# Scores in groups of eight and values in groups of eight once the maxima are through, in a gated mix of linear and softmax attention

## The chip, the cores and the metric

The kernel runs on one core of a Trainium2 chip. The metric is the device time of one execution, in microseconds (us). The kernel before takes 1025.13 us, the median of 3 runs (1024.96 to 1025.58). The engines are named as the profile names them: PE is TensorE (matmuls; PEld are its weight loads), DVE is VectorE, ACT is ScalarE, POOL is GpSimd, and SP is SyncE, whose queue issues the DMA transfers (SPq).

## The reference, cut to what matters

```python
B, S, D, H = 1, 2048, 448, 16          # Dh = 28

def _A_ref(x, wqkv, w_phi, wo):        # linear attention with learned features
    q, k, v = split(x @ wqkv)
    pq, pk = q @ w_phi, k @ w_phi      # per head
    phi_q = concat([softmax(pq), softmax(-pq)])
    phi_k = concat([softmax(pk), softmax(-pk)])
    kv, z = phi_k.T @ v, phi_k.sum(over s)
    return heads_joined((phi_q @ kv) / (phi_q @ z + 1e-6)) @ wo

def _B_ref(x, wqkv, wo):               # full softmax attention
    q, k, v = split(x @ wqkv)
    p = softmax(q @ k.T * Dh ** -0.5)
    return heads_joined(p @ v) @ wo

g = sigmoid((x * gate_w).sum(-1, keepdims=True))
out = g * _A_ref(x, A_wqkv, A_w_phi, A_wo) + (1 - g) * _B_ref(x, B_wqkv, B_wo)
```

All inputs and the output are 32-bit floats. The change touches only the second half of the softmax attention (B) and its output projection.

## The kernel before, in words

The first 440 us or so compute the projections of x, the linear attention A with its output (kept in DRAM as `gad`, one block of 512 tokens each), the values of B (`vb`), and the queries and keys of B, which are stored in DRAM (`qkd`).

Then comes the long loop at the end of the function, over steps `s`. A step is one tile of 128 keys (`kt`, 16 of them) for one block `gq` of four heads and 512 queries: `g` counts four groups of four heads, `qb` four blocks of queries, `gq = 4 g + qb`. There are 256 steps (`NS`). A step has these parts, in this order on TensorE:

- Scores (`scores`, L865): four matmuls of 128x128 against 128x512, one per head (L871). Each writes a PSUM bank of its own, taken from the list `free`; when a step's four are issued, its banks go back to the list's end. ScalarE then takes the exponential of each bank (L889) into a tile `p`; `p` has eight buffers, two steps' worth.
- Values (`values`, L991) of the step before: per head a 32-column matmul on the exponentials (L998). A 32-bit product takes two passes, so these are eight matmuls of 128x32 against 128x512, in two groups of four that run side by side on the four column quarters of the array. They add into one bank, `pv`, over the block's 16 steps. A column of ones among the values gives the sum of the exponentials.
- Maxima (`mx_visit`, L304): a step's share of the row maxima of later blocks (L321, four matmuls), read by ScalarE (L325) and VectorE (L329, L332). They are through at step 212. Until then their query and key tiles (`qc`, `kc`, from `mx_tile`, L178) are in use; after that they are idle. `spare_open` (L942) then returns their banks and keeps one, the spare, for projections, so that scores cycle through six.

A finished block goes through `finish` (L1035), called with the number `s` of the step at which the block's last values are issued. `f1` at once: VectorE copies `pv` (L398), SP sends the sums' rows to a small tile (L401). `f2` at `s + 3`: VectorE takes the reciprocals (L408), SP writes them to DRAM (L412) and reads them back spread over the partitions (L413). `f3` at `s + 8`: GpSimd multiplies (L419). `f4` at `s + 9`, issued at the next step's start: GpSimd splits the result into a high and a low part (L427, L428); for the first three groups of heads SP stores them (L1055, `od`).

When the last group of heads of a query block is through (blocks 12, 13, 14), its 512 tokens are projected in four pieces (`project`, L1003): eight passes on the stored heads of the other groups (`first_passes`, L1013), then three on the fresh ones (`out_passes`), eleven matmuls of 128x128 against 128x448 (L108) into the spare bank; VectorE adds the gated result (L1009) and SP sends it (L1011). The pieces are issued at steps `s + 10` to `s + 13`, that is 218 to 221, 234 to 237 and 250 to 253, behind the step's values. The stored heads are loaded by `load_out` (L951), seven DMA issues at the steps in `OUTS`: blocks 0, 1 and 2 share one buffer (`oL`), block 3 has the idle buffer `kst[1]` and a tile `oLl`. Block 15, the last, is finished in the tail (`tail_open`, `tail_fill`, `finish_last`, from L1019 on).

The order of the work on TensorE, VectorE, ScalarE and GpSimd is the order in which the code is written. SP's queue is ordered by a planner at build time: it places a DMA issue as soon as, by its reckoning, what the issue needs is ready, and among several that are ready it takes the one that stands first in the code. A transfer can thus be issued many steps ahead of its place. At run time SP works through its queue in order.

The loop's lines that the change rewrites:

```python
            if s:
                scores(s, 0)
                scores(s, 1)
        ...
        if 0 < s <= NS:
            values(s - 1)
```

Of the kernel before, what the change touches and what calls it, by code (L numbers as in the profile page):

```python
# [8 lines left out]
F32 = mybir.dt.float32  # L9
# [8 lines left out]
P = 128  # L18
# [5 lines left out]
NG = 4  # L24
NT = S // P
NQ = S // 512
# [2 lines left out]
NU = NG * NQ * 16  # L29
NF = 44  # L30
LOWEST = -3.0e38
OUTS = (200, 222, 242, 206)


def f32(ap):
    return ap.bitcast(F32)
# [3 lines left out]
def gated_mix_kernel(ctx, tc, xT, wqkB, wvB, wvA, wkAT, wqAT, phi, woA, woB,  # L40
# [26 lines left out]
    def ps_mx(nm, d):  # L67
        return ps.tile([P, 2, 512], F32, tag="md" if d and psn[1] == 3 else "mx", name=nm,
                       bufs=1 if d and psn[1] == 3 else 2)
# [36 lines left out]
    def run(dst, todo):  # L106
        for i, (l, r) in enumerate(todo):
            nc.tensor.matmul(dst, l, r, start=i == 0, stop=i == len(todo) - 1)  # L108
# [48 lines left out]
    acts = []  # L157
# [6 lines left out]
    def take_acts():  # L164
        while acts:
            acts.pop(0)()
# [11 lines left out]
    def mx_tile(tag, nm, bufs):  # L178
        return mxp.tile([P, 512], F32R, tag=tag, name=nm, bufs=bufs)
# [214 lines left out]
    def normalize1(pool, pn, nm, n):  # L394

        oU = pool.tile([P, n, 512], F32, tag="oU", name=f"oU{nm}", bufs=1 + n)
        for i in range(n):
            (nc.scalar.copy if n == 2 else nc.vector.tensor_copy)(oU[:, i, :], pn[i])  # L398
        den = pool.tile([P, n, 16], F32, tag="den", name=f"den{nm}", bufs=2)
        for i in range(n):  # L400
            nc.sync.dma_start(den[:, i, :], oU[DH:P:32, i, :])  # L401
        return oU, den
# [29 lines left out]
    def out_passes(oT, c, w, g):  # L432
        tt = slice(c, c + P)
        return [(oT[:, 0, tt], w[:, 0, g, :]), (oT[:, 0, tt], w[:, 1, g, :]),
                (oT[:, 1, tt], w[:, 0, g, :])]
# [290 lines left out]
    for i in range(2 * NT + 11):  # L726
        t, q = i, i - NT
# [132 lines left out]
        kst_of[(g, kb)] = load_stack(kst[(4 * g + kb) % 5], k_d[g], kb * 512, (0, 1, 0, 1))  # L860

    NS = NG * NQ * NT
    pv_of, pts, late, mids = {}, {}, {}, {}

    def scores(s, i):  # L865

        gq, kt = divmod(s, NT)
        g, qb = divmod(gq, NQ)

        def score(j, st):  # L870
            nc.tensor.matmul(st, kst_of[(g, kt // 4)][:, j, (kt % 4) * P:(kt % 4 + 1) * P],  # L871
                             qst_of[gq][:, j, :], start=True, stop=True)

        if s == 0:
            p = at.tile([P, 2, 512], F32, name=f"p{s}_{i}")
            st = ps_mx(f"st{s}_{i}", i)
            for jl in range(2):
                score(2 * i + jl, st[:, jl, :])
            nc.scalar.activation(p, st, AF.Exp, scale=SCALE)
            pts.setdefault(s, []).extend([p[:, 0, :], p[:, 1, :]])  # L880
            return
        sts = []
        for j in (2 * i, 2 * i + 1):
            used.append(free.pop(0))
            sts.append(bank(used[-1], f"st{s}_{j}"))
            score(j, sts[-1])
        for st in sts:
            p = late_p.tile([P, 512], F32, tag="p", name=f"p{s}_{len(pts.get(s, []))}", bufs=8)
            nc.scalar.activation(p, st, AF.Exp, scale=SCALE)  # L889
            pts.setdefault(s, []).append(p)  # L890
        if i == 1:
            a, m = used[:], held[:]
            free.extend([a[0], m[0], a[1], m[1], a[2], a[3], m[2]] if m else a)
            used.clear()
            held.clear()
# [33 lines left out]
    free, used, held = list(range(7)), [], []  # L929
    spare = []  # L930

    def bank(i, nm):
        return ps2.tile([P, 512], F32, tag=f"g{i}", name=nm, bufs=1)
# [8 lines left out]
    def spare_open():  # L942
        free.extend(held)
        held.clear()
        spare.append(free.pop())

    late_p = ctx.enter_context(tc.tile_pool(name="late", bufs=1, reuse_waits="tile"))
    woB_s = late_p.tile([P, 2, 4, D], F32R, name="woB_s")
# [2 lines left out]
    def load_out(qb):  # L951


        if qb < NQ - 1:
            o = late_p.tile([P, NG - 1, 2, 512], F32R, tag="oL", name=f"oL{qb}", bufs=1)
            oL_of[qb] = [o[:, b] for b in range(NG - 1)]
        else:
            o = kst[(4 * NG) % 5]
            oL_of[qb] = [o[:, 0:2], o[:, 2:4],
                         late_p.tile([P, 2, 512], F32R, tag="oLl", name="oLl", bufs=1)]  # L960
        tt = slice(qb * 512, (qb + 1) * 512)
        for b in range(2):
            nc.sync.dma_start(f32(oL_of[qb][b]), o_d[b * P:(b + 1) * P, :, tt])
        r = oL_of[qb][2]
        for i in range(2):
            nc.sync.dma_start(f32(r[:80, i, :]), o_d[256:336, 0, tt])
        nc.sync.dma_start(f32(r[80:, 0, :]), o_d[288:336, 1, tt])
        nc.sync.dma_start(f32(r[80:96, 1, :]), o_d[288:304, 1, tt])
        nc.sync.dma_start(f32(r[96:, 1, :]), o_d[256:288, 1, tt])
# [33 lines left out]
    def project(qb, oT, tl):  # L1003

        t = qb * 4 + tl
        acc = acc_of[qb][:, tl, :]
        po = bank(spare[0], f"pob{t}")
        run(po[:, :D], first_passes(qb, tl) + out_passes(oT, tl * P, woB_s, NG - 1))
        nc.vector.scalar_tensor_tensor(acc, po[:, :D], gate1[:, t:t + 1], acc,  # L1009
                                       op0=ALU.mult, op1=ALU.add)  # L1010
        nc.sync.dma_start(out[0, t * P:(t + 1) * P, :], acc)  # L1011

    def first_passes(qb, tl):  # L1013
        o, tt = oL_of[qb], slice(tl * P, (tl + 1) * P)
        return [x for b in range(2) for x in out_passes(o[b], tl * P, woB_s, b)] + [
            (o[2][:, i, tt], woB_s[:, i, 2, :]) for i in range(2)]
# [3 lines left out]

    def tail_open():
        tail["po"] = [bank(i, f"poL{n}")[:, :D]
                      for n, i in enumerate([spare[0], free.pop(0), free.pop(0)])]
        for tl in range(4):
            tail["todo"] += [(tl, i == 0, x) for i, x in enumerate(first_passes(NQ - 1, tl))]

# [8 lines left out]
    def finish(gq, s):  # L1035

        st = {}
        g, qb = divmod(gq, NQ)
        last = gq == NG * NQ - 1

        def f1():
            st["n"] = normalize1(late_p, [pv_of[gq]], f"b{gq}", 1)

        def f2():
            st["n"] = normalize2(late_p, *st["n"], f"b{gq}", 1, False)

        def f3():
            st["n"] = normalize3(*st["n"], 1)

        def f4():  # L1050
            st["o"], = normalize4(late_p, st["n"], f"b{gq}", 1)
            if g < NG - 1:
                for j in range(4):
                    r = (4 * g + j) * DH
                    nc.sync.dma_start(o_d[r:r + DH, :, qb * 512:(qb + 1) * 512],  # L1055
                                      f32(st["o"][32 * j:32 * j + DH]))

        if last:
            finish_last(gq)
            return  # L1060
        f1()
        late.setdefault(s + 3, []).append(f2)
        late.setdefault(s + 8, []).append(f3)
        late.setdefault(s + 9, []).append(lambda: acts.append(f4))
        if g == NG - 1:
            for tl in range(4):
                mids[s + 10 + tl] = lambda tl=tl: project(qb, st["o"], tl)

    def finish_last(gq):

# [43 lines left out]

    for s in range(NS + 16):
        take_acts()
        if s < NS:
            gq, kt = divmod(s, NT)
            g, qb = divmod(gq, NQ)
            if s in (0, 3):  # L1120
                load_k(0, 2 + s // 3)
            if g + 1 < NG and qb == NQ - 1 and kt % 4 == 2:
                load_k(g + 1, kt // 4)
            if kt == 12 and gq + 1 < NG * NQ:
                load_q(gq + 1)
            if kt == (12 if gq + 1 < 14 else 14) and gq + 1 < NG * NQ - 1:
                load_nm(gq + 1)
            if s in OUTS:
                load_out(OUTS.index(s))
            if g == NG - 1 and kt == 8:  # L1130
                load_acc(qb)
            if s:
                scores(s, 0)
                scores(s, 1)
        if s == NS:
            tail_open()
            tail_fill(3)
        if 0 < s <= NS:
            values(s - 1)
            if s % NT == 0:  # L1140
                finish(s // NT - 1, s)
        if s:
            mx_visit()
        if mxs["f"] == len(flats):
            mx_fin()
        if s in mids:
            mids.pop(s)()
        if mxs["f"] == len(flats) and not spare:
            spare_open()
        if NG * NQ - 1 in nm_of and NG * NQ - 1 in qst_of:  # L1150
            load_nm(NG * NQ - 1)
        for fn in late.pop(s, []):
            fn()
# [68 lines left out]
```

## Time and profile before

| what | us |
|---|---|
| median of 3 runs | 1025.13 |
| the profiled execution | 1025.96 |
| its span | 1024.2 |
| step 213's scores begin | 889.80 |
| step 214's scores begin | 891.97 |
| first projection's matmuls begin | 902.57 |
| tail begins (first matmul of L1032) | 1007.91 |
| last matmuls of scores before the tail begin | 1005.79 |

The span is the time from the first to the last instruction of the profiled execution. Busy time of PE is modelled: matmuls are pipelined, and a row's length includes its way through the array, so the distance between the starts of two rows says more than their lengths. A row of the timeline is start, length, engine, line, operation, output and inputs, shapes, count, and in brackets the idle time before it on that engine with what ended it.

### The profile page before, as it was taken

The numbers are of one execution on the slowest core, as the hardware profiler recorded it, in microseconds if no ns is written. First come the engines' busy times: TensorE is split into PE (matmuls) and PEld (weight loads), VectorE is DVE, ScalarE is ACT, GpSimd is POOL, SyncE is SP. The second block draws the span as 40 slices with busy tenths as digits, with TensorE's granted clock in tenths as the row PEclk, the third lists the DMA queues.
The fourth block names the chain that finished last, engine by engine and source line by source line (L and its number), as shares of the span: only waits on it lengthen the run. The fifth ranks groups of instructions, "written<-read, shape, count | busy, mean of one in ns | idle before, by whom it ended". The sixth has DMA issues, their size and how long they took to land.

```text
span 1024.2 us, 18042 instructions
## 1 busy us (share of the span) xinstructions
PE 1013.9 (99%) x6472; PEld 557.3 (54%) x6472; DVE 680.7 (66%) x1340; ACT 820.0 (80%) x1534; POOL 236.2 (23%) x213
## 2 busy tenths in 40 slices
PE   9999999999999999999999999999999999999998
PEld 8878888868779433333333333333333333354555
DVE  6566567987753588788888787887878887710102
ACT  5445445677752999999999999999999999969672
POOL 1245546678435003111011110101201101011010
PEclk9999999989999999999999999999999999999999
DMA  8973110132345713233532133522313355414401
GB/s 297 310 238 93 52 52 1 61 73 81 94 129 132 146 26 77 69 68 72 123 79 72 42 74 74 128 58 55 89 42 77 87 129 140 121 58 125 132 32 54
DMA packets 64250, 98.89 MB, mean 97 GB/s; under 512 B 18176, under 2 KB 24944, under 8 KB 64160
## 3 DMA queue, kind: packets, MB, share of 16 engines
q1 hardware_dynamic: 64160, 97.74, 35.4%
q8 instruction: 51, 0.84, 0.4%
q14 instruction: 39, 0.32, 0.1%
HBM read 69.54 MB, written 27.78 MB: 95 GB/s over the span
## 4 chain that ended last, share of the span: by engine, by line
PE 89%; DVE 4%; DMA 4%; ACT 1%; SPq 1%; issue 1%; POOL 0%; DVEq 0%; ACTq 0%; POOLq 0%
PE st L871 29%; PE pv L998 25%; PE pm L321 9%; PE pk L126 4%; PE pva L126 4%; PE poa L108 4%; PE pob L108 3%; PE pq L108 2%; PE pqk L108 2%; DMA qkd<-ev 2%; PE pvb L126 2%; PE pvb L108 2%; PE pmb L284 1%; PE pft L524 1%; DVE rl L289 1%; DMA wvA_raw<-in_wvA_dram 1%
## 5 line engine op out<-in xcount | busy, mean ns | idle before, releaser
L889 ACT ACTIVATE p<-st 128x512 f32<-128x512 f32 x1020 | 525.7, 609 | 29.5 <-PE st L871 27.9
L332 DVE TENSOR_REDUCE part<-pm 128x1 f32<-128x512 f32 x477 | 304.8, 686 | 111.1 <-PE pm L321 104.7
L871 PE MATMUL st<-qst,kst 128*128 128x512 f32 x1024 | 315.5, 430 | 0.5 <-ACT vb L714 0.5
L998 PE MATMUL pv<-p,vb 128*32 128x512 f32 x2048 | 272.7, 605 | 0.0
L871 PEld LDWEIGHTS st<-qst,kst 128*128 128x128 f32 x1024 | 173.0, 187 | 137.5 <-issue 75.8
L321 PEld LDWEIGHTS pm<-kc,qc 28*128 28x128 f32 x848 | 40.5, 181 | 177.8 <-ACT p L889 169.4
L325 ACT ACTIVATE rl<-pm 128x512 f32<-128x512 f32 x212 | 126.9, 599 | 11.0 <-PE pm L321 0.3
L419 POOL TENSOR_TENSOR oUb<-oUb,rsb 128x512 f32<-128x512 f32 x15 | 19.3, 1289 | 467.4 <-DMA rsb<-rdb 229.9
L329 DVE CUSTOM_DVE_ANT_0 rl<-pm,rl 128x512 f32<-128x512 f32 x159 | 108.3, 681 | 0.0
L321 PE MATMUL pm<-kc,qc 28*128 28x512 f32 x848 | 107.1, 495 | 0.0
L998 PEld LDWEIGHTS pv<-p,vb 128*32 128x32 f32 x2048 | 40.3, 108 | 67.3 <-issue 63.1
L289 DVE CUSTOM_DVE_ANT_0 rl<-pmb,rl 128x512 f32<-128x512 f32 x88 | 57.1, 686 | 29.4 <-ACT rl L287 29.4
L1009 DVE SCALAR_TENSOR_TENSOR acc<-pob,gate,acc 128x448 f32<-128x448 f32 x12 | 8.2, 684 | 86.2 <-PE pob L108 86.2
L108 PE MATMUL pqk<-XH,wB 128*128 128x512 f32 x192 | 59.3, 397 | 0.0
L287 ACT ACTIVATE rl<-pmd 128x1024 f32<-128x1024 f32 x44 | 45.2, 1028 | 12.2 <-PE pmd L284 5.6
L588 ACT CAST ev<-pqk 128x512 fp32r<-128x512 f32 x28 | 16.1, 588 | 36.1 <-PE pqk L108 30.2
L108 PE MATMUL poa<-woA_s,oTa 128*128 128x448 f32 x192 | 43.2, 374 | 0.0
L108 PEld LDWEIGHTS pqk<-XH,wB 128*128 128x128 f32 x192 | 35.4, 188 | 8.5 <-issue 1.5
L108 PE MATMUL pq<-wqA_s,XH 128*128 128x448 f32 x128 | 38.1, 381 | 0.8 <-DVE ev L589 0.8
L195 POOL TENSOR_TENSOR kc<-kc,kd 28x512 fp32r<-28x512 f32 x12 | 15.4, 1281 | 101.9 <-PE pm L321 50.7
L108 PEld LDWEIGHTS poa<-woA_s,oTa 128*128 128x128 f32 x192 | 35.1, 188 | 6.0 <-issue 3.3
L589 DVE TENSOR_TENSOR ev<-pqk,ev 128x512 fp32r<-128x512 f32 x28 | 19.0, 690 | 28.4 <-ACT ev L588 28.3
(159 smaller groups left out, 1176.8 us busy)
## 6 DMA issues: line engine op xcount, KB each, us to landing
qkd<-ev SPq DMA_DIRECT2D x28, 512.0 KB
qst<-qkd SPq DMA_DIRECT2D x64, 224.0 KB
kst<-qkd SPq DMA_DIRECT2D x64, 224.0 KB
od<-oTb SPq DMA_DIRECT2D x48, 112.0 KB
rsa<-rda SPq DMA_DIRECT2D x8, 512.0 KB
rsb<-rdb SPq DMA_DIRECT2D x15, 256.0 KB
kc<-qkd SPq DMA_DIRECT2D x64, 56.0 KB
gad<-ga SPq DMA_DIRECT2D x16, 224.0 KB
```

The lines of the kernel that those rows point to most:

```text
L108: nc.tensor.matmul(dst, l, r, start=i == 0, stop=i == len(todo) - 1)
L126: nc.tensor.matmul(dst[:, :n], l, r, start=i == 0, stop=i == len(todo) - 1, skip_group_check=True)
L287: nc.scalar.activation(rl, pd, AF.Relu)
L289: nc.vector.tensor_tensor_reduce(rl[:, i, :], pb[:, i, :], rl[:, i, :], 1.0, LOWEST, ALU.add, ALU.max, part[:, col + i:col + i + 1])
L321: nc.tensor.matmul(pm[j], mxs[("qc", gq)][js, qt * P:(qt + 1) * P], mxs[("kc", g, kb)][js, :], start=True, stop=True, tile_position=(32 * ...
L325: nc.scalar.activation(rl, pm[kb], AF.Relu if kb < 3 else AF.Copy)
L329: nc.vector.tensor_tensor_reduce(r, pm[j], r, 1.0, LOWEST, ALU.add, ALU.max, part[:, col + j:col + j + 1])
L332: nc.vector.tensor_reduce(part[:, col + j:col + j + 1], pm[j], AX.X, ALU.max)
L419: (nc.gpsimd if n == 1 else nc.vector).tensor_mul(oU, oU, rs)
L871: nc.tensor.matmul(st, kst_of[(g, kt // 4)][:, j, (kt % 4) * P:(kt % 4 + 1) * P], qst_of[gq][:, j, :], start=True, stop=True)
L889: nc.scalar.activation(p, st, AF.Exp, scale=SCALE)
L998: nc.tensor.matmul(pv[32 * j:32 * j + 32, :], vb[kt // 8][:, kt % 8, 4 * g + j, :], pt[j], start=kt == 0, stop=kt == NT - 1, tile_position ...
```

## The change

`TWO` is 213, the first step after the last maxima. Up to step 212 nothing is different in the order of scores and values. From step 213 on:

- An odd step issues its own scores and those of the next step, eight matmuls in a row; an even step issues none. Values stay as they were, one step's at each step, so that on TensorE eight scores are followed by two steps' values. The last step, 255, has only its own four.
- The exponentials of odd steps use the tiles `p` as before. Those of even steps use the maxima's idle tiles: `kc` (five buffers) for steps divisible by four, and three of `qc` (three buffers) with one of `kc` for the other even steps.
- No bank is kept as a spare: scores cycle through seven banks. A projection takes the next bank of the same list and puts it at the list's end; the tail takes its banks from the list too.
- The projections are issued at every second step: 218, 220, 222, 224 for block 0, 234 to 240 for block 1, 248 to 254 for block 2, each behind the second of two steps' values.
- For blocks that finish from step 213 on, `f2` is issued at `s + 2` in place of `s + 3`, `f3` and `f4` at `s + 5` in place of `s + 8` and `s + 9`.
- `load_out`: block 1 at step 227 in place of 222, block 2 at 206 in place of 242, block 3 at 243 in place of 206. Block 2 now has the buffers that block 3 had (`kst[1]` and `oLl`), and blocks 0, 1 and 3 share `oL`.

```diff
-OUTS = (200, 222, 242, 206)
+OUTS = (200, 227, 206, 243)
+PROJ = (218, 234, 248)
...
+    TWO = NG * NQ * 16 - NF + 1
...
-        for st in sts:
-            p = late_p.tile([P, 512], F32, tag="p", name=f"p{s}_{len(pts.get(s, []))}", bufs=8)
+        for j, st in enumerate(sts, 2 * i):
+            if s < TWO or s % 2:
+                p = late_p.tile([P, 512], F32, tag="p", name=f"p{s}_{j}", bufs=8)
+            else:
+                tag = "qc" if s % 4 and j < 3 else "kc"
+                p = f32(mx_tile(tag, f"p{s}_{j}", 3 if tag == "qc" else 5))
             nc.scalar.activation(p, st, AF.Exp, scale=SCALE)
...
     def spare_open():
         free.extend(held)
         held.clear()
-        spare.append(free.pop())
+        spare.append(1)
...
-        if qb < NQ - 1:
+        if qb != 2:
             o = late_p.tile([P, NG - 1, 2, 512], F32R, tag="oL", name=f"oL{qb}", bufs=1)
...
-        po = bank(spare[0], f"pob{t}")
+        free.append(free.pop(0))
+        po = bank(free[-1], f"pob{t}")
         run(po[:, :D], first_passes(qb, tl) + out_passes(oT, tl * P, woB_s, NG - 1))
...
         tail["po"] = [bank(i, f"poL{n}")[:, :D]
-                      for n, i in enumerate([spare[0], free.pop(0), free.pop(0)])]
+                      for n, i in enumerate([free.pop(0) for _ in range(3)])]
...
         f1()
-        late.setdefault(s + 3, []).append(f2)
-        late.setdefault(s + 8, []).append(f3)
-        late.setdefault(s + 9, []).append(lambda: acts.append(f4))
+        d2, d3, d4 = (3, 8, 9) if s < TWO else (2, 5, 5)
+        late.setdefault(s + d2, []).append(f2)
+        late.setdefault(s + d3, []).append(f3)
+        late.setdefault(s + d4, []).append(lambda: acts.append(f4))
         if g == NG - 1:
             for tl in range(4):
-                mids[s + 10 + tl] = lambda tl=tl: project(qb, st["o"], tl)
+                mids[PROJ[qb] + 2 * tl] = lambda tl=tl: project(qb, st["o"], tl)
...
-            if s:
-                scores(s, 0)
-                scores(s, 1)
+            for z in ([s] if s < TWO else [s, s + 1][:NS - s] if s % 2 else []):
+                if z:
+                    scores(z, 0)
+                    scores(z, 1)
```

## The prediction

> **What bounds the kernel now.** I read the page first (engines, slices, chain), then busy time by stretch, then the order of time on TensorE.
>
> ```profile
> span 1024.2 us, 18042 instructions
> PE 1013.9 (99%) x6472; PEld 557.3 (54%) x6472; DVE 680.7 (66%) x1340; ACT 820.0 (80%) x1534; POOL 236.2 (23%) x213
> ACT  5445445677752999999999999999999999969672
> PE 89%; DVE 4%; DMA 4%; ACT 1%; SPq 1%; issue 1%; POOL 0%; DVEq 0%; ACTq 0%; POOLq 0%
> ```
>
> TensorE carries the chain; ScalarE is full from slice 14 to slice 35 and falls off after that, in the stretch that the change rewrites. The stretches (columns: length, then busy time and count of PE, PEld, DVE, ACT, POOL, granted clock, DMA):
>
> ```profile
> 820.00:889.36 69.36, 69.36 (x427) 26.87 (x425) 56.69 (x114) 68.03 (x135) 3.20 (x3) 1.00 0.52 132
> 902.57:920.01 17.44, 17.44 (x97) 11.58 (x93) 2.74 (x4) 8.26 (x18) 0.00 (x0) 1.00 0.16 55
> 926.39:945.47 19.08, 19.08 (x113) 7.48 (x109) 0.25 (x1) 18.59 (x38) 3.20 (x3) 1.00 0.42 112
> ```
>
> The first still has maxima. The second is four steps, each with a projection: ScalarE works less than half of it. The third is nine steps without one: 2.12 us each, and ScalarE looks full (18.59 of 19.08). So the question for the plain steps is whether TensorE or ScalarE sets the 2.12. The rows of TensorE answer it:
>
> ```profile
> 925.39 1.06 PE L998 MATMUL pv<-p,vb 128*32 128x512 f32 x8
> 925.85 0.61 PE L998 MATMUL pv<-p,vb 128*32 128x512 f32 x4
> 926.39 1.19 PE L871 MATMUL st<-qst,kst 128*128 128x512 f32 x4
> 926.72 0.63 PE L871 MATMUL st<-qst,kst 128*128 128x512 f32 x2
> 927.18 0.40 PE L871 MATMUL st<-qst,kst 128*128 128x512 f32 x1
> 927.51 0.16 PEld L998 LDWEIGHTS pv<-p,vb 128*32 128x32 f32 x8 [0.37 <-issue]
> 927.51 1.06 PE L998 MATMUL pv<-p,vb 128*32 128x512 f32 x8
> 928.51 1.19 PE L871 MATMUL st<-qst,kst 128*128 128x512 f32 x4
> ...
> 1007.91 0.88 PE L1032 MATMUL poL<-woB_s,kst 128*128 128x448 f32 x3
> ```
>
> Rows with x1, x2 or x4 are the rest of a group, from a window that opens inside it. Scores begin at 926.39; the second at 926.72 (0.33), the fourth at 927.18 (0.23 each); the values at 927.51 (0.33 after the fourth score). The values are two groups of four: the second begins 0.46 after the first (925.39, 925.85), and the scores 0.54 after that. So TensorE never waits for an exponential here, yet each change between scores and values costs something: 0.10 at the first score, 0.10 at the first values, 0.08 behind the last values. ScalarE alone would be faster:
>
> ```profile
> 905.40 2.07 ACT L889 ACTIVATE p<-st 128x512 f32<-128x512 f32 x4 [2.29 <-PE st L871]
> 980.75 4.03 ACT L889 ACTIVATE p<-st 128x512 f32<-128x512 f32 x8 [0.34 <-PE st L871]
> ```
>
> Eight exponentials without a pause take 4.03 us from the first start to the last end; four take 2.07, so four more cost 1.96, 0.49 each at most (0.48 if the last, queued longest, is counted longer). Two steps of ScalarE are 3.84 to 3.92 us, two of TensorE 4.24. TensorE binds; little stands behind it.
>
> **The change, part by part.**
>
> Pairs. From step 213 on, an odd step issues its own four scores and the next step's four, then come two steps' values. Steps 213 to 254 are 21 pairs, 255 stays single. Of a pair: four scores after values 1.12 (926.39 to 927.51), four more at 0.23 = 0.92; values 3 x 0.46 + 0.54 = 1.92. Sum 3.96 against 2 x 2.12 = 4.24: 0.28 saved per pair, 21 x 0.28 = 5.9 us. Values straight behind values stand nowhere in the trace. The bounds are 0.46 (as the second group follows the first) and 0.54 (as the scores follow): a saving of 0.28 or 0.20. I take 0.46, since the nearest row is the same instruction: all eight weight loads of 927.51 are through in 0.16 us, beside running matmuls.
>
> ScalarE in a pair: 3.84 to 3.92 against 3.96, so it follows by a hair. The second values of a pair need the exponentials of the pair's first four scores, which are issued in the same pair. With the rows of the next fence, the first exponential starts 0.49 after the first score behind a projection, 0.59 behind values, and four end 2.07 later: 2.66. Those values are due at 2.04 + 0.92 = 2.96. Slack 0.3 us; nothing.
>
> Banks. Eight scores cycle through seven banks (the projection's own bank is given to the cycle): the eighth score, at about 1.74, needs the first exponential's end, 0.59 + 0.60 = 1.2. Nothing. A projection takes the next bank of the cycle, read for 0.7 us by VectorE; scores meet it again seven banks later. Nothing.
>
> Buffers of the exponentials: even steps write into the maxima's idle tiles, four steps before reuse; the same ACTIVATE, the same cost.
>
> Projections: twelve as before, one per pair and behind values, as before.
>
> ```profile
> 914.66 1.06 PE L998 MATMUL pv<-p,vb 128*32 128x512 f32 x8
> 915.65 1.89 PE L108 MATMUL pob<-woB_s,oL 128*128 128x448 f32 x8
> 917.38 0.78 PE L108 MATMUL pob<-woB_s,oTb 128*128 128x448 f32 x3
> 918.00 1.08 PE L871 MATMUL st<-qst,kst 128*128 128x512 f32 x4
> 918.49 3.69 ACT L889 ACTIVATE p<-st 128x512 f32<-128x512 f32 x7 [2.30 <-PE st L871]
> 919.01 1.06 PE L998 MATMUL pv<-p,vb 128*32 128x512 f32 x8
> ```
>
> A projection holds TensorE 2.35 us and spares the next score its 0.10: 2.24 net, from the 17.44 us above: (17.44 - 4 x 2.12) / 4. The order values, projection, scores stays, so this term does not move. Check of both terms: the scores of step 214 begin at 891.97 (next fence), and 42 x 2.12 + 12 x 2.24 = 115.9 us later is 1007.9, where the trace has the tail's first matmul (1007.91). No step of this stretch waits.
>
> The join at step 213. The second four scores now come while VectorE still reads the last maxima:
>
> ```profile
> 889.80 1.24 PE L871 MATMUL st<-qst,kst 128*128 128x512 f32 x4
> 889.92 1.29 DVE L332 TENSOR_REDUCE part<-pm 128x1 f32<-128x512 f32 x2 [0.55 <-PE pm L321]
> 891.13 0.68 DVE L329 CUSTOM_DVE_ANT_0 rl<-pm,rl 128x512 f32<-128x512 f32 x1
> 891.97 1.19 PE L871 MATMUL st<-qst,kst 128*128 128x512 f32 x4
> ```
>
> The seventh score would start at about 889.80 + 0.33 + 5 x 0.23 = 891.3; its bank is read until 891.8. Loss 0.5 us, once (bounds 0 and 1.0, one more VectorE operation).
>
> Sums and transfers. The projection of block 14 now comes sooner: from step 240's values to its last three passes lie one projection 2.35, a pair 3.86, three pairs 11.88, eight passes 1.73, together 19.8 us, less 0.25 to VectorE's copy: 19.6. Block 13 has one pair more: 23.5. The work it needs, as it stands:
>
> ```profile
> 924.51 0.69 DVE L398 COPY oUb<-pv 128x512 f32<-128x512 f32 x1 [5.63 <-PE pv L998]
> 941.22 1.29 POOL L428 TENSOR_TENSOR oTb<-oUb,oTb 128x512 fp32r<-128x512 f32 x1
> ...
> 967.40 0.69 DVE L398 COPY oUb<-pv 128x512 f32<-128x512 f32 x1 [5.63 <-PE pv L998]
> 970.34 0.34 SPq L412 DMA_DIRECT2D rdb<-denb  x1
> 974.35 0.57 SPq L413 DMA_DIRECT2D rsb<-rdb  x1
> 981.52 1.29 POOL L428 TENSOR_TENSOR oTb<-oUb,oTb 128x512 fp32r<-128x512 f32 x1
> ```
>
> 18.0 us for block 13 (924.51 to 942.51) and 15.4 for block 14. Both fit, with 5.5 and 4.2 to spare (1.6 for block 14 at block 13's length). What moves on SP's queue: a load of stored heads is seven issues. Block 1's goes from step 222 to 227, block 3's comes at 243 in place of block 2's at 242, block 2's takes block 3's early place and buffers. SP issues what is ready, ahead of its place:
>
> ```profile
> 917.57 0.59 SPq L963 DMA_DIRECT2D oL<-od  x1
> 922.05 0.42 SPq L969 DMA_DIRECT2D oL<-od  x1
> ...
> 889.40 0.35 SPq L412 DMA_DIRECT2D rdb<-denb  x1
> 890.87 0.60 SPq L413 DMA_DIRECT2D rsb<-rdb  x1
> 892.05 1.74 SPq L857 DMA_DIRECT2D qst<-nm  x2
> ```
>
> First and last of seven; the buffer came free at 917.4, the end of the last projection's first eight passes. In the new kernel it comes free at the fourth projection, right behind the values whose sums are to be sent, so these transfers meet. The sums' write took 4.0 us to be answered behind large loads (970.34 to 974.35) and 1.47 without (889.40 to 890.87). On VectorE the reciprocal now stands behind the read of that projection, 0.3 us later than before; behind the waiting sums on SP stand loads and results that are wanted eight steps on. I cost the meeting at 2.5 us within the slack, so nothing; its ends are nothing and seven issues, 7 x 0.6 = 4.2, with 2.5. Queries' maxima, wanted one step earlier now, were on their way at 892.05 for scores 30 us later: nothing. The earlier steps of GpSimd (+5 for +8 and +9) only change order in a queue with nothing else in it: nothing. The tail has the same passes: nothing.
>
> Sum: 5.9 - 0.5 = 5.4 us. The profiled execution took 1025.96 us, 1.8 around its span, and lies 0.83 above the median 1025.13; it would come to 1020.6, the median to 1019.7.
>
> **The rivals.**
>
> B, loads between the two values show. If the second step's first weight loads must wait for the running matmuls, it follows at 0.54: 0.20 x 21 - 0.5 = 3.7 us, 1021.4. Against it: the 0.16 us for eight loads, four of them for the second group. For it: nothing in the trace is this case. The Trainium skill ("TensorE: Matmul & The Clock Gate", Part 3, What overlaps and what doesn't) says that a weight load runs beside matmuls in flight only where the row group differs; all values have all rows, so by that rule B would hold. The row of 927.51 speaks against it.
>
> C, ScalarE becomes the bound. In the stretch with maxima it did 135 operations in 69.36 us, 0.514 each and 98% busy. Eight at 0.52 are 4.16: nine pairs without a projection then save 0.08, twelve with one keep 0.28 (ScalarE has over 2 us idle there): 0.7 + 3.4 - 0.5 = 3.6, 1021.5. Against it: eight in a row at 0.48 to 0.49. The Trainium skill ("ScalarE: Activation LUTs", What ACT_TABLE_LOAD costs) gives 186 ns + 0.833 ns an element less an overlap of 93, an estimate of 0.52 us for 512 elements, which would make C hold; the run of eight disagrees.
>
> D, the other side: the projection of block 14 waits for its sums. If the seven loads stand ahead of the sums on SP and their data ahead in the DMA engines, the 15.4 us become 15.4 + 4.2 + 2.5 = 22.1, or 24.7 from block 13's 18.0: a wait of 2.5 to 5.1 us on TensorE, 1022.2 to 1024.8. It decides from 25.0 us on (19.6 + 5.4): then the kernel is slower than before. For it: loads and sums now become ready together. Against it: slack, and steps that put the sums first.
>
> **How the numbers follow.** A change of less than 0.2% (2.05 us) can hardly be told from none: faster is below 1023.1, slower above 1027.2. My forecast 0.62 (its own range 1019.2 to 1020.3, from a join of 0 to 1.0), B 0.12, C 0.08, D 0.13 (0.03 of it faster by over 0.2%, 0.05 within, 0.05 slower), and 0.05 for what I don't see, split 0.02, 0.01, 0.02. Faster 0.62 + 0.12 + 0.08 + 0.03 + 0.02 = 0.87, same 0.06, slower 0.07. The range 1019.0 to 1022.2 takes in the forecast, with the 0.2 us by which the runs shown fall below their median, B, C and D's lower end.
>
> **What would show it.** Right: pairs of 3.96 us and pairs with a projection of 6.2, second values 0.46 behind the first, ScalarE at 8 in 3.9. B: 4.04 and 0.54. C: score or values loads waiting for ScalarE, plain pairs of 4.16. D: TensorE idle before the last three passes of a projection, at block 14 first, and SP's row for the sums later than 4 us behind VectorE's copy. The prediction is wrong if any pair waits for something I put inside slack.

## The result and the profile after

The changed kernel takes 1019.01 us, the median of six runs (1018.4 to 1019.32), against 1025.12 us for the kernel before (six runs). The ratio is 0.9936, with a 95% interval of 0.9925 to 0.9948 (the quotient of the two medians, 0.9940, lies inside it): 5.3 to 7.7 us faster. The forecast was 5.4 us, 1019.7 us in a range of 1019.0 to 1022.2. The direction and the place were right, the amount too small: the median lies on the range's lower edge, and 1025.13 times the ratio is 1018.6, below it.

The page's first lines and its chain, which answer to those of before:

```profile
span 1017.1 us, 18036 instructions
PE 1006.6 (99%) x6472; PEld 563.0 (55%) x6472; DVE 682.1 (67%) x1340; ACT 817.2 (80%) x1534; POOL 236.4 (23%) x213
ACT  5445445677753899999999999999999999978682
PE 92%; DVE 4%; DMA 1%; ACT 1%; issue 1%; SPq 0%; POOL 0%; DVEq 0%; ACTq 0%; POOLq 0%
```

The span is 7.1 us shorter. In this execution step 213's scores begin at 889.47 (before: 889.80), a third of a microsecond from the front of the kernel, where nothing was changed. From there to the tail's first matmul it takes 111.37 us (rounded rows: 889.47 to 1000.85) in place of 118.11 (889.80 to 1007.91), so the rewritten stretch gives 6.7 us.

```profile
1000.85 0.88 PE L1039 MATMUL poL<-woB_s,oL 128*128 128x448 f32 x3
```

I call this length the stretch below; it leaves out the front, the launch and the tail. The tail is 16.3 us long in both kernels; the front differs from run to run (step 213's scores begin between 888.30 and 891.20 in the profiled runs whose front is that of before), by more than some of the effects below.

Busy time by stretch, after (columns as in the prediction): four pairs with projections, and four pairs without.

```profile
901.86:926.31 24.45, 24.45 (x144) 16.02 (x141) 3.59 (x6) 16.12 (x33) 0.00 (x0) 1.00 0.20 62
926.31:941.94 15.63, 15.63 (x101) 7.76 (x97) 0.00 (x0) 15.63 (x33) 3.19 (x3) 1.00 0.79 200
```

A pair with a projection takes 24.45 / 4 = 6.11 us, a plain pair 15.63 / 4 = 3.91. Before, two plain steps took 4.24 and a projection came on top with 2.24, so plain pairs save 0.33 and those with a projection 0.37. ScalarE's row in the plain pairs is full, 15.63 of 15.63; whether it binds is for the experiments.

Where the forecast of 3.96 and 6.20 went wrong shows in the rows of one pair (order of time on TensorE; x4 and x8 are what is left of a group in a window that opens inside it):

```profile
928.38 0.16 PEld L1004 LDWEIGHTS pv<-p,vb 128*32 128x32 f32 x8 [0.36 <-issue]
928.38 1.92 PE L1004 MATMUL pv<-p,vb 128*32 128x512 f32 x16
928.83 0.56 PEld L1004 LDWEIGHTS pv<-p,vb 128*32 128x32 f32 x8 [0.30 <-issue]
928.83 1.04 PE L1004 MATMUL pv<-p,vb 128*32 128x512 f32 x8
929.26 1.04 PE L1004 MATMUL pv<-p,vb 128*32 128x512 f32 x8
929.69 0.61 PE L1004 MATMUL pv<-p,vb 128*32 128x512 f32 x4
930.23 2.11 PE L873 MATMUL st<-qst,kst 128*128 128x512 f32 x8
```

The four groups of values start at 928.38, 928.83, 929.26 and 929.69: 0.45, then 0.43 and 0.43; the scores 0.54 after the last. Only the first distance in a row of values is longer; I read that as the weight loads of its first group, which have no values to run beside, but no run separates them. The loads of the second step's first group (the third of the four) are in the row at 928.83, while matmuls run, and the distance to that group is 0.43, as it is to the fourth. So sixteen values take 1.85 us, not 1.92. Eight scores took 2.04 to 2.07 (928.38 less 926.31), as forecast.

The join cost more than forecast. Its rows (loads of scores, with what they waited for, and VectorE's last read of a bank):

```profile
889.47 2.81 PE L873 MATMUL st<-qst,kst 128*128 128x512 f32 x8
890.22 0.32 PEld L873 LDWEIGHTS st<-qst,kst 128*128 128x128 f32 x2 [0.21 <-ACT rl L326]
890.81 0.68 DVE L330 CUSTOM_DVE_ANT_0 rl<-pm,rl 128x512 f32<-128x512 f32 x1
890.95 0.19 PEld L873 LDWEIGHTS st<-qst,kst 128*128 128x128 f32 x1 [0.41 <-DVE part L333]
891.55 0.30 PEld L873 LDWEIGHTS st<-qst,kst 128*128 128x128 f32 x2 [0.42 <-DVE part L330]
892.21 1.92 PE L1004 MATMUL pv<-p,vb 128*32 128x512 f32 x16
```

Two scores wait for VectorE, not one, and the values begin 2.74 us after the first score in place of 2.04: 0.70 us. The wait that ends last sets this, and it is the one of the forecast: VectorE's read ends at 891.49, 0.54 after the seventh score was due (889.47 + 0.33 + 5 x 0.23 = 890.95). The seventh's weights are loaded only after that, from 891.55, and the values follow 0.66 later in place of 0.56. The sixth score's wait was over by 890.95 and is hidden behind it.

### The profile page after: what moved, and what is told of

Same layout as the page of the kernel before. It is cut to its first block, busy times and chain, and to the rows that moved or that the text cites. A ratio compares the mean times of both kernels' runs of the same rounds, so it can differ in the third digit from the quotient of the medians.

```text
span 1017.1 us, 18036 instructions
## 1 busy us (share of the span) xinstructions
PE 1006.6 (99%) x6472; PEld 563.0 (55%) x6472; DVE 682.1 (67%) x1340; ACT 817.2 (80%) x1534; POOL 236.4 (23%) x213
## 4 chain that ended last, share of the span: by engine, by line
PE 92%; DVE 4%; DMA 1%; ACT 1%; issue 1%; SPq 0%; POOL 0%; DVEq 0%; ACTq 0%; POOLq 0%
PE st L873 29%; PE pv L1004 25%; PE pm L322 9%; PE pqk L109 5%; PE pk L127 4%; PE pva L127 4%; PE pob L109 3%; PE poa L109 3%; PE pq L109 2%; PE pvb L127 2%; PE pvb L109 1%; PE pmb L285 1%; PE pqk L652 1%; DMA dena<-oUa 1%; PE pft L525 1%; DVE fsumq L459 1%
## 5 line engine op out<-in xcount | busy, mean ns | idle before, releaser
L873 PE MATMUL st<-qst,kst 128*128 128x512 f32 x1024 | 310.2, 427 | 0.6 <-ACT vb L715 0.5
L1004 PE MATMUL pv<-p,vb 128*32 128x512 f32 x2048 | 268.4, 604 | 0.0
L420 POOL TENSOR_TENSOR oUb<-oUb,rsb 128x512 f32<-128x512 f32 x15 | 19.4, 1291 | 464.1 <-DMA rsb<-rdb 192.6
L1004 PEld LDWEIGHTS pv<-p,vb 128*32 128x32 f32 x2048 | 44.4, 108 | 70.2 <-issue 62.0
L196 POOL TENSOR_TENSOR kc<-kc,kd 28x512 fp32r<-28x512 f32 x12 | 15.4, 1281 | 101.3 <-PE pm L322 60.2
```

What stands on the lines that cost most here:

```text
L420: (nc.gpsimd if n == 1 else nc.vector).tensor_mul(oU, oU, rs)
L1004: nc.tensor.matmul(pv[32 * j:32 * j + 32, :], vb[kt // 8][:, kt % 8, 4 * g + j, :], pt[j], start=kt == 0, stop=kt == NT - 1, tile_position ...
```

## Experiments

Theory 1 was that each change on TensorE between scores, values and projections has its price, and that the kernel gained the changes that went. Rivals: the seventh bank carries the gain (2), ScalarE binds the plain pairs (3), the order of transfers on SP matters (4). The kernel before has medians of 1025.12, 1026.14 and 1026.59 us on the three chips used; the ratios are each against the kernel before on the same chip.

### A projection between a pair's two values

```diff
-PROJ = (218, 234, 248)
+PROJ = (219, 235, 249)
```

> The changed kernel with each projection between a pair's two values (steps 219, 221, 223, 225 and so on) in place of behind them. If every change of kind on TensorE has its price (theory 1: the gain is the removed changes between scores and values), a pair with a projection goes from 6.11 us (8 scores 1.92, 16 values 1.85, projection 2.34) to 2.04 + 1.00 + 2.34 + 1.00 = 6.38, or 6.47 if the values behind a projection pay 0.09 as they do behind scores: 12 x 0.27 to 0.36 = 3.2 to 4.3 us slower than the changed kernel, about 1022.2 to 1023.3. If the gain comes from the seventh bank (theory 2), nothing moves: 1019.0.

Ratio 0.9968 (0.9955 to 0.9981), stretch 115.41 us: 4.04 more than the changed kernel, at the upper end of theory 1. The rows:

```profile
902.75 1.07 PE L1004 MATMUL pv<-p,vb 128*32 128x512 f32 x8
903.75 1.90 PE L109 MATMUL pob<-woB_s,oL 128*128 128x448 f32 x8
905.49 0.77 PE L109 MATMUL pob<-woB_s,oTb 128*128 128x448 f32 x3
906.19 1.07 PE L1004 MATMUL pv<-p,vb 128*32 128x512 f32 x8
907.18 2.11 PE L873 MATMUL st<-qst,kst 128*128 128x512 f32 x8
909.23 1.06 PE L1004 MATMUL pv<-p,vb 128*32 128x512 f32 x8
```

Values to projection 1.00, projection to values 2.44 (0.10 more than to scores, whose shape it shares), values to scores 0.99, eight scores 2.05: 6.48 us in place of 6.11. Eleven of the twelve projections stand so (behind the last come matmuls of the tail, of the same shape), and 11 x 0.37 = 4.1. The work and its amount are the same; only the order is not. The second theory predicted no change and falls as the whole explanation.

### Six banks in place of seven

```diff
-        spare.append(1)
+        spare.append(free.pop())
...
-        free.append(free.pop(0))
-        po = bank(free[-1], f"pob{t}")
+        po = bank(spare[0], f"pob{t}")
...
-                      for n, i in enumerate([free.pop(0) for _ in range(3)])]
+                      for n, i in enumerate([spare[0], free.pop(0), free.pop(0)])]
```

> The changed kernel with the spare bank kept for the projections, so that eight scores cycle through six banks. Theory 1 (changes of kind): the eighth score, due 1.74 us after the first, needs the second exponential's end at 0.59 + 0.49 + 0.60 = 1.68, so at most 0.1 us a pair, 0 to 2 us slower than the changed kernel (1019.0 to 1021.0). Theory 2 (the seventh bank carries the gain): most of it goes back, 1023 or more.

Ratio 0.9957 (0.9940 to 0.9973), stretch 113.90 us: 2.5 more. The eighth score's load waits for an exponential in every pair behind the join:

```profile
927.48 2.24 PE L873 MATMUL st<-qst,kst 128*128 128x512 f32 x8
929.21 0.19 PEld L873 LDWEIGHTS st<-qst,kst 128*128 128x128 f32 x1 [0.28 <-ACT p L895]
929.65 1.92 PE L1004 MATMUL pv<-p,vb 128*32 128x512 f32 x16
```

Eight scores take 2.17 (927.48 to 929.65), 0.13 longer, a little above the bound of 0.1; the join is 0.36 shorter (the last maxima's bank is the one kept). The seventh bank is what lets groups of eight run without a wait; alone it should give nothing, since before, from step 214 on, no score was held up by a bank; that kernel was not run.

### One exponential in eight less, and one more

```diff
         for j, st in enumerate(sts, 2 * i):
+            if s >= TWO and s % 2 == 0 and j == 3:
+                pts[s].append(pts[s][2])
+                continue
```

> The changed kernel without every eighth exponential from step 214 on (the fourth head of the even steps; the third head's is used twice). If TensorE binds the pairs (theory 1), plain pairs stay at 3.90 us and pairs with a projection at 6.11, 1019.0 in all. If ScalarE binds the plain pairs (theory 3), each gets shorter by up to 0.4 us down to what TensorE needs: nine of them, up to 3.6 us, 1015.4.

```diff
-            nc.scalar.activation(p, st, AF.Exp, scale=SCALE)
+            for _ in range(2 if s >= TWO and s % 2 == 0 and j == 3 else 1):
+                nc.scalar.activation(p, st, AF.Exp, scale=SCALE)
```

> The changed kernel with one exponential more in each pair (the fourth head of the even steps, written twice). ScalarE then has nine in a pair, 9 x 0.478 = 4.30 us. Theory 1 (TensorE binds at 3.90, ScalarE has under 0.1 us to spare): plain pairs go to about 4.30, 9 x 0.40 = 3.6 us; pairs with a projection (6.11) hide it; about 1022.6. Theory 3 (ScalarE binds already): plain pairs grow by the full 0.48, 4.3 us, about 1023.3. If ScalarE had ample room, nothing would change.

One less: 1019.21 us, stretch 111.43, the same plain pairs. One more: 1022.40 us, stretch 115.82 (one run each). The four plain pairs with one less, then rows of plain pairs with one more, with two exponentials of ScalarE:

```profile
926.55:942.18 15.63, 15.63 (x100) 7.76 (x96) 0.00 (x0) 14.15 (x29) 3.19 (x3) 1.00 0.80 201
```

```profile
925.81 2.35 PE L873 MATMUL st<-qst,kst 128*128 128x512 f32 x8
928.08 2.09 PE L1005 MATMUL pv<-p,vb 128*32 128x512 f32 x16
930.11 2.61 PE L873 MATMUL st<-qst,kst 128*128 128x512 f32 x8
932.64 2.08 PE L1005 MATMUL pv<-p,vb 128*32 128x512 f32 x16
934.65 1.66 PE L873 MATMUL st<-qst,kst 128*128 128x512 f32 x6
...
930.35 0.69 ACT L896 ACTIVATE p<-st 128x512 f32<-128x512 f32 x1
931.07 0.60 ACT L896 ACTIVATE p<-st 128x512 f32<-128x512 f32 x1
```

With less work ScalarE is busy 14.15 of 15.63 us and the time is the same: TensorE binds the plain pairs, and theory 3 falls. With more, the first plain pair behind a projection takes 4.30 (925.81 to 930.11), a plain pair behind another 4.54 (930.11 to 934.65), and pairs with a projection stay at 6.1. ScalarE had little to spare: eight exponentials at 0.478 us from start to start are 3.82 of a pair's 3.91. 4.54 is more than nine times 0.478 (4.30) because the additional operation writes the same tile again and waits for the first write: it starts at 931.07, when that one has ended (930.35 + 0.69 = 931.04), so 0.72 behind its start in place of 0.48. With this wait the experiment cannot weigh theory 1 against theory 3 by the size of the loss; the first one, with less work, decides.

### Pairs from step 215 on

```diff
-    TWO = NG * NQ * 16 - NF + 1
+    TWO = NG * NQ * 16 - NF + 3
```

> The changed kernel with pairs from step 215 on (steps 213 and 214 single, 20 pairs). Theory 1: the join waits for the last maxima's banks; there the first eight scores take 2.74 us in place of 2.04. With two single steps between, this wait of 0.70 is gone and one pair's saving (0.34) with it: the stretch from step 213's scores to the tail goes from 111.37 us to about 111.0. If the wait at the join has another cause (say the banks of step 212's exponentials), it moves to step 215 and the stretch gets longer, about 111.7.

The stretch is 111.12 us, 0.25 less than the changed kernel's 111.37. Step 213's scores take 1.17, step 214's 1.12, and the first eight 2.04 (894.83 to 896.87):

```profile
894.83 2.11 PE L873 MATMUL st<-qst,kst 128*128 128x512 f32 x8
896.87 1.92 PE L1004 MATMUL pv<-p,vb 128*32 128x512 f32 x16
```

So the wait at the join is the last maxima's banks, and it goes when two single steps stand between. By its stretch this is the best version here; the one run of the whole (1019.71 us, on a chip where the kernel before had 1026.59) cannot tell a difference of 0.25 us.

### The stored heads' loads ahead of the sums

```diff
-OUTS = (200, 227, 206, 243)
+OUTS = (200, 225, 206, 241)
```

> The changed kernel with the loads of stored heads ahead of the sums' transfers in the code (steps 225 and 241 in place of 227 and 243). In the changed kernel block 14's projection has its sums 1.7 us before it needs them, block 13's 3.8. If the order on SP matters (theory 4), up to seven issues of 0.6 us go ahead of the sums, 4.2 us: block 14 waits up to 2.5 us, block 13 up to 0.4, so 1019.0 to 1022. If the order does not matter (the data wait in the DMA engines anyway, or the planner keeps the order), no wait: 1019.0.

Ratio 0.9957 (0.9943 to 0.9972), stretch 113.43 us: 2.06 more. Rows of block 14, SP's above all, first the changed kernel, then this one (`denb` is the sums' first transfer, `rdb` their write, `rsb` their spreading, `oL` the stored heads):

```profile
960.56 0.69 DVE L399 COPY oUb<-pv 128x512 f32<-128x512 f32 x1 [3.17 <-PE pv L1004]
961.28 0.61 SPq L402 DMA_DIRECT2D denb<-oUb  x1
962.19 0.60 SPq L969 DMA_DIRECT2D oL<-od  x1
964.33 0.33 SPq L413 DMA_DIRECT2D rdb<-denb  x1
967.78 0.58 SPq L414 DMA_DIRECT2D rsb<-rdb  x1
...
976.90 1.28 POOL L429 TENSOR_TENSOR oTb<-oUb,oTb 128x512 fp32r<-128x512 f32 x1
979.86 0.77 PE L109 MATMUL pob<-woB_s,oTb 128*128 128x448 f32 x3
```

```profile
966.96 0.42 SPq L975 DMA_DIRECT2D oL<-od  x1
967.49 0.36 SPq L413 DMA_DIRECT2D rdb<-denb  x1
967.89 0.43 SPq L995 DMA_DIRECT2D acc<-gad  x1
973.73 0.59 SPq L414 DMA_DIRECT2D rsb<-rdb  x1
...
980.75 0.67 PE L109 MATMUL pob<-woB_s,oTb 128*128 128x448 f32 x2 [0.70 <-POOL oTb L428]
982.11 0.47 PE L109 MATMUL pob<-woB_s,oTb 128*128 128x448 f32 x1 [0.69 <-POOL oTb L429]
```

All seven issues of the load now stand ahead of the write, in place of one (967.49 in place of 964.33), and the write's answer takes 6.2 us in place of 3.5. Block 14's projection waits for its sums, 4.25 us in place of 2.34, and block 13's 0.1. This is rival D of the prediction, in a kernel one line away.

### The pairs alone

The kernel before with the loop, `TWO` and the tiles `p` of the changed kernel, and nothing else:

```diff
-        for st in sts:
-            p = late_p.tile([P, 512], F32, tag="p", name=f"p{s}_{len(pts.get(s, []))}", bufs=8)
+        for j, st in enumerate(sts, 2 * i):
+            if s < TWO or s % 2:
+                p = late_p.tile([P, 512], F32, tag="p", name=f"p{s}_{j}", bufs=8)
+            else:
+                tag = "qc" if s % 4 and j < 3 else "kc"
+                p = f32(mx_tile(tag, f"p{s}_{j}", 3 if tag == "qc" else 5))
...
-            if s:
-                scores(s, 0)
-                scores(s, 1)
+            for z in ([s] if s < TWO else [s, s + 1][:NS - s] if s % 2 else []):
+                if z:
+                    scores(z, 0)
+                    scores(z, 1)
```

> The kernel before with the pairs alone: eight scores, two steps' values, the maxima's tiles for even steps; the spare bank kept (six banks), projections at four steps in a row, the sums' steps and the loads as before. Theory 1, from the runs so far: six banks cost 2.5 us against the changed kernel's stretch, and two projections of each block now stand between a pair's values, 6 x 0.34 = 2.0 us: a stretch of about 115.9, 2.2 us less than before (118.1), so about 1023 on the scale of 1025.1 before. If the pairs alone carried everything, the stretch would be 111.4 (1019.0).

Ratio 0.9981 (0.9968 to 0.9994), stretch 115.86 us: 2.25 less than before, as worked out from the first two experiments (115.9). A third of the gain is in the pairs as such; two thirds, by the prices of those two experiments, need the seventh bank (2.5) and the projections behind the pairs (2.0).

### Values paired while the maxima run

```diff
+    px = late_p.tile([P, 4, 512], F32, tag="oL", name="px", bufs=1)
+    PV = 197
...
-            if s < TWO or s % 2:
+            if s < PV and s % 3 == 2:
+                p = px[:, j, :]
+            elif s < TWO or s % 2:
...
-            values(s - 1)
+            for z in ([s - 1] if s >= PV else [s - 2, s - 1] if s % 2 == 0 else []):
+                values(z)
```

> The changed kernel, and two steps' values behind one another also while the maxima run (steps 1 to 196: an even step issues both, an odd step none; a third of the exponentials' tiles comes from the buffer that the stored heads take from step 200 on). Scores and maxima keep their order. Theory 1 (changes of kind on TensorE): 16 values take 1.85 us in place of 2 x 1.00, 98 pairs x 0.14 = 13.7 us faster than the changed kernel, about 1005, if ScalarE (ten operations of 0.48 in 5.2 us) and the seven banks follow. Theory 5: while TensorE is at two steps' values, ScalarE and VectorE run out of full banks, and TensorE waits for them afterwards; the gain is lost, 1019 or more.

Ratio 1.0598 (1.0578 to 1.0618), 1087.57 us. Theory 5 holds, by far more than I had thought:

```profile
702.47 0.50 PE L322 MATMUL pm<-kc,qc 28*128 28x512 f32 x4
702.91 1.25 PE L873 MATMUL st<-qst,kst 128*128 128x512 f32 x4
704.15 0.99 PE L322 MATMUL pm<-kc,qc 28*128 28x512 f32 x4
704.64 0.18 PEld L322 LDWEIGHTS pm<-kc,qc 28*128 28x128 f32 x2 [0.30 <-ACT px L897]
705.13 1.48 PE L873 MATMUL st<-qst,kst 128*128 128x512 f32 x4
706.54 1.07 PE L1008 MATMUL pv<-p,vb 128*32 128x512 f32 x8
707.42 1.04 PE L1008 MATMUL pv<-px,vb 128*32 128x512 f32 x8
708.39 0.51 PE L322 MATMUL pm<-kc,qc 28*128 28x512 f32 x4
```

The values do take 1.85 (706.54 to 708.39). But two steps' scores and maxima, sixteen results, now stand in a row before them, on seven banks: the second maxima take 0.98 in place of 0.44 and the scores behind them 1.41 in place of 1.17, waiting for banks that ScalarE has not read. Just before, ScalarE had stood idle for 0.92 us and VectorE for 2.21, both until the row's first maxima (702.47). Two steps take 5.92 us (702.47 to 708.39) where the trace of before has 2.61 a step, and 98 times the difference of 0.7 is about 69 us, the size of the loss (1.0598 against 0.9936, 68 us).

## Why the prediction was right or wrong

- *What binds.* Right: TensorE in both kinds of steps, ScalarE behind it by under 0.1 us in the plain ones (3.82 of 3.91). Taking an exponential away changed nothing, adding one cost time.
- *Pairs, 0.28 each, 5.9 us.* This is the term that was mis-sized. I gave each group of values after the first 0.46, the distance from a step's first group to its second, and called 0.46 and 0.54 the bounds. That distance is longer only behind the first group of a row; between later groups it is 0.43, across the steps too. The trace of before had a hint in the rows' modelled lengths: 0.64 us for the first four, 0.61 for the second. Sixteen values therefore take 1.85, not 1.92; some 0.02 of this is rounding, since the unrounded first distance is 0.453 before and after. By the stretches above, a plain pair is 0.05 shorter than I worked out (3.96) and one with a projection 0.09 (6.20): 9 x 0.05 + 12 x 0.09 = 1.5 us, of which the values are 21 x 0.066 = 1.4. The error in the stretch is 1.3 (112.7 worked out, 111.4 measured), as the join took 0.2 back. Rival B (0.54) was farther off still. The rule of the Trainium skill that I weighed there ("TensorE: Matmul & The Clock Gate", Part 3, What overlaps and what doesn't) is not borne out here: loads of the same row group run beside matmuls at 928.83. The Trainium skill ("TensorEngine Tiling (Array Packing)", Tiling Modes, Key Properties) states that a change of tiling mode drains the engine; the 0.10 to 0.11 us that each change costs in these rows agree with that, though no run here shows what they are made of.
- *Projections, 2.24 each, unchanged.* Right within 0.04: 2.34 before scores that are 0.12 to 0.15 shorter, 2.20 net (6.11 less 3.91).
- *Banks, nothing.* Right with seven behind the join; with six it would have been 0.13 a pair.
- *The join, 0.5.* Measured 0.70. The bank and its reader were right. I left out what follows the read: the score's weights are loaded only then, and 0.16 us more went by. The other wait for VectorE, which I did not see, costs nothing beside it. The runs with six banks and with the join two steps later show the same cause: there the values begin 2.38 and 2.04 behind the first score.
- *Rival C, 0.52 an exponential.* Did not come: plain pairs run eight in 3.91 us. The 0.52 us that I estimated from the Trainium skill ("ScalarE: Activation LUTs", What ACT_TABLE_LOAD costs) is above the 0.478 from start to start of the changed kernel's trace. By the row that I gave beside it (0.514 each) eight would have been 4.11, not 4.16.
- *Sums and transfers, nothing within 4.2 us of slack.* Right. Block 14's path from VectorE's copy at 960.56 to 978.18 took 17.6 us, where I had 15.4 and 2.5 for the meeting of loads and sums, and was 1.7 us early (its passes begin at 979.86); block 13's took 19.4 and was 3.8 early. With the loads first it waited 1.9 us, a little under rival D's 2.5 to 5.1.
- *The range.* Its floor came from the same 0.46. As 0.46 was no bound, the floor was no floor; that the median of these runs still lies on it is chance.

## What to carry to other kernels

When one engine runs several kinds of work in turns, count the changes of kind, price each from the distances between starts, and then look for buffers that allow longer rows of one kind; the row's length is set by how many results can wait unread, as six against seven banks and the failed pairing beside the maxima show. A distance measured at the head of a row is not the distance inside it: where the trace has no such inside, the distance at the head is no lower bound, and the forecast's range has to stay open on that side. Where a transfer's order is left to readiness, the line that says which comes first can be worth a third of the change itself (2.06 us of 6.7 here).

## What I had not expected of the hardware

Weight loads of 32-column matmuls ran wholly inside the time of the group ahead, across steps too (0.43 us between groups, 0.45 at the head). A small write whose answer is awaited took 1.5 us with no load shortly ahead, 3.5 behind one issue of a large load and 6.2 behind all seven on the same queue.
